# Shifted matmuls in place of a strided load, unit 0's means on VectorE, and longer planned landing times in an interleaved conv and FFN kernel

## Chip, cores, metric

One Trainium2 chip, one core of it. The metric is device time in microseconds of one execution of the whole program, from HBM inputs to HBM output; the time before is the median of 3 runs, 932.0 us (931.72 to 933.56). The profiled execution is one more run, of 932.73 us; its span, from the first to the last instruction of the trace, is 930.9 us.

## What is computed

Two layers, each a gated causal convolution (A) and a gated feed-forward block (B), each with a residual and a layer norm ahead of it, on S = 2048 tokens of D = 576 channels, with F = 4608 hidden units and 4 taps in the short convolution:

```python
def A(q, k, v, shift_k, ssm_k, ssm_D):
    k_pad = jnp.pad(k, ((0, 0), (ks - 1, 0), (0, 0)))
    k_shift = sum(k_pad[:, t:t + S, :] * shift_k[:, ks - 1 - t] for t in range(ks))
    kv = k_shift * v
    y = irfft(rfft(kv padded to 2S) * rfft(ssm_k padded to 2S))[:S]
    y = y + kv * ssm_D
    return q * y

def B(x, w_gate, w_up, w_down):
    return (gelu(x @ w_gate) * (x @ w_up)) @ w_down

x = A_q
x = x + A(layernorm(x), A_k, A_v, A_shift_k, A_ssm_k, A_ssm_D)
x = x + B(layernorm(x), B_w_gate, B_w_up, B_w_down)
x = x + A(layernorm(x), A_k, A_v, A_shift_k, A_ssm_k, A_ssm_D)
x = x + B(layernorm(x), B_w_gate, B_w_up, B_w_down)
```

The convolution's `y` does not depend on `x`, so both layers share it. All inputs and the output are bfloat16.

## The kernel before, in words

**Units.** The tokens are cut into four chunks of 512. A unit is one chunk in one layer: (layer 0, chunk 0), (0, 1), (1, 0), (1, 1), then the same of chunks 2 and 3, numbered 0 to 7. The weights are streamed in five passes over units [0], [1, 2], [3, 4], [5, 6], [7], and each pass has three phases, one per third of F. One visit of a unit in a phase is 12 up-projections `gu` (gate and up side by side, 18 matmuls each, L1435; GELU on ScalarE L1439, product into `hT` on VectorE L1440) and then four down-projections `dn` (L1452), one for each tile of 128 rows, added to the residual `x_c` on VectorE (L1488). Tokens lie on partitions as (p i): partition p holds the four consecutive tokens 4p to 4p+3.

**Convolution.** It is done in blocks of 512 tokens by a Fourier transform written as matmuls with twiddle tables `W` and `Wx`. Per block: load `k` and `v` (`load_k` L168, `load_v` L173); multiply the shifted keys by the taps on VectorE (`kvt`, L186 and L191) and by `v` (L196); transform (L222 and L260 on TensorE, `eo` on ScalarE, L237 to L251 on VectorE); multiply the spectra `kr` (of kv) and `hr` (of the filter), which are spilled to DRAM (`Kd`, `Hd`, L349) and loaded again (L459, L467), with L297 to L301; transform back (L339). The filter block is turned by DMA transposes (L369), written to DRAM (`Td`) and read again (L388).

**The head (`begin`).** Block 0 of the convolution and the first chunk's norm run before the first `gu`, in an order written out by hand. SP issues, in this order: `k`, `kx`, the filter's first block `hn` in two parts (L719, L720), `v`, `x_b` (the first chunk's input, L1006), half of the twiddles `W` (L736), `Wx`, the filter's second block, the other half of `W`, then the first FFN weights `wgu` (L991 to L993). ACT's queue issues `sk` and `dvec` (the taps and the skip weights). For the first 512 channels of block 0 the taps are applied by TensorE: `k` is transposed into `kT` (L769, evicted L771) and multiplied by diagonal matrices `dg` made from the taps (`shift_taps`, L662), and VectorE multiplies the PSUM result by `v` (L779). For the last DW = 64 channels (`taps_rest`) VectorE does it all, from `kx`: seven rows per partition, of which rows 3 to 6 are the partition's own four tokens (copied at L784) and rows 0 to 2 are the three tokens ahead of them, which are the last three tokens of partition p - 1. They come by a strided load of 127 x 3 pieces of 64 channels (L727). Partition 0 has zeros there (L724).

PSUM tiles in the head come from `ps()`, which gives three tiles of the pool `psp` and then one of the single-buffered `cpsp`, in turn.

**Unit 0's norm.** `gate0` makes the first layer's gated sum and its row sum `s` (L1288, L1291 on VectorE), `mean0` the negated mean `nm` (GpSimd, L1051, through `mean_after`), `sq0` the sum of squares (ScalarE, L1059), `root0` the reciprocal root `rstd` (GpSimd, L1066 and L1067), `norm0` the normalized tile `xn` (L1241), `turn0` its transposes (L1257) and `copy0` the eviction into `xnT` (L1264), which the first `gu` reads (L1360). Tiles 0 and 2 go first, 1 and 3 between the first half-width `gu`.

**The plan.** Everything else of the convolution and the norms is placed between the FFN's matmuls at build time. `Pace` counts a planned time for TensorE (`t.pe`), VectorE and ScalarE from the constants `C_*`; `fill` takes from the queues `L` (loads), `V` (VectorE operations), `Pq` (TensorE pieces) and `spills` whatever is ready at the planned time. A load is taken to have landed a fixed number of microseconds after its planned issue: `at["k"]` and `at["v"]` (9.0 each), `at[("ld", kt, a)]` for `kr` and `hr` (8.0), `hd_at` for a spilled spectrum (6.0). An operation is emitted no earlier than that. The emitted order is fixed; on the chip each engine takes its instructions in that order and waits on semaphores. The loads and spills above all go through GpSimd's queue, the weights and transposes through SP's.

Of the kernel before, what the change touches and what calls it, by code (L numbers as in the profile page):

```python
# [16 lines left out]
ALU = mybir.AluOpType  # L17
F32 = mybir.dt.float32
BF16 = mybir.dt.bfloat16
# [3 lines left out]
P = 128  # L23
# [3 lines left out]
RT = BS // P  # L27
# [57 lines left out]
class Conv:  # L85
# [261 lines left out]
    def spill(self, dst, t, ready=0.0, key=None):  # L347
        def run():
            self.nc.gpsimd.dma_start(out=dst, in_=t[:].rearrange("p s d -> p (s d)"))  # L349
            self.hd_at[key] = self.t.pe + 6.0  # L350
        self.spills.append((ready, run))

    def store(self, dst, t, ready):
# [57 lines left out]
    def step(self, m, kv=None, loaded=False):  # L411

        nc, D, t = self.nc, self.D, self.t
        kc, kr, hr, z, nyb, prs = {}, {}, {}, {}, {}, {}
        KTS = (0, 2, 1, 3)
        at = {}
# [5 lines left out]
        if not loaded:  # L422
            def lk():
                self.load_k(m, nc.gpsimd)
                at["k"] = t.pe + 9.0

            def lv():
                self.load_v(m, nc.gpsimd)
                at["v"] = t.pe + 9.0
            self.L.append((lambda: max(self.kv_at.get(m - 1, NEVER), self.td_at.get(self.NB - 1, NEVER)), lk))  # L430
            self.L.append((lambda: self.filt_at.get(m, NEVER), lv))
        else:
            at["k"] = at["v"] = 0.0
# [19 lines left out]
        def load(kt, a):  # L453
            def run():
                if a < m:
                    kr[(kt, a)] = (self.nkr % 3, self.krp.tile([P, 2, D], BF16, tag="kr", name="kr"))
                    self.kr_free[self.nkr % 3] = NEVER
                    self.nkr += 1
                    nc.gpsimd.dma_start(out=kr[(kt, a)][1][:].rearrange("p s d -> p (s d)"), in_=self.Kd[a][kt])  # L459
                if m == 1 and a == 0:  # L460
                    hr[(kt, a)] = (None, self.H1[:, kt, :, :])
                    at[("ld", kt, a)] = t.pe + 8.0
                    return
                hr[(kt, a)] = (self.nhr % N_HR, self.hrp.tile([P, 2, D], BF16, tag="hr", name="hr"))
                self.hr_free[self.nhr % N_HR] = NEVER
                self.nhr += 1
                nc.gpsimd.dma_start(out=hr[(kt, a)][1][:].rearrange("p s d -> p (s d)"), in_=self.Hd[m - a][kt])  # L467
                at[("ld", kt, a)] = t.pe + 8.0
            return run
        for kt, a in pairs:  # L470
            self.L.append((lambda a=a: max(self.hr_free[self.nhr % N_HR] if (m, a) != (1, 0) else 0.0,
# [120 lines left out]
        def inv(mt):  # L592
            def run():
                self.yb = nyb
                self.inverse(m, mt, self.terms(mt, z))
                done = t.on_act(C_EVA, t.pe + 0.98 + LAG)
                self.ps_free = done + LAG
                self.y_at[(m, mt)] = done + LAG
            return run
        zs = get(*[("z", kt, part) for kt in range(2) for part in range(2)])  # L600
        self.z_at[m] = zs
        out = [(lambda: max(zs(), self.y_used.get(m - 2, NEVER) if m > 1 else 0.0), 0.98, inv(mt), m) for mt in range(RT)]
# [92 lines left out]
    def begin(self, head, tables):  # L695

        tc, nc, D, KS = self.tc, self.nc, self.D, self.KS
        nd = D // P
        width = lambda db: min(P, D - db * P)
        with ExitStack() as es:  # L700
            tmp = es.enter_context(tc.tile_pool(name="s_tmp", bufs=1))
# [10 lines left out]
            dg = head.scratch([P, nd, RT, P], "dg")  # L712
            DW = D - nd * P
            kx = tmp.tile([P, RT + KS - 1, DW], BF16, name="kx")
            wx = [tmp.tile([P, RT, DW], BF16, name=f"wx{i}") for i in range(2)]

            def load_h(b):
                cols = slice(b * BS, (b + 1) * BS)
                nc.sync.dma_start(out=hn[b][:, 0:nd, :], in_=self.hk[0:nd * P, cols].rearrange("(b p) t -> p b t", p=P))  # L719
                nc.sync.dma_start(out=hn[b][0:D - nd * P, nd, :], in_=self.hk[nd * P:D, cols])  # L720

            nc.scalar.dma_start(out=sk1[:].rearrange("p d j -> p (d j)"), in_=self.sk.rearrange("d j -> (d j)").unsqueeze(0))
            self.load_k(0, nc.sync)
            nc.vector.memset(kx[:, 0:KS - 1, :], 0.0)  # L724
            base = self.k2[RT - KS + 1:RT - KS + 2, nd * P:nd * P + 1]
            row = base.ap[0][0]
            nc.sync.dma_start(out=kx[1:P, 0:KS - 1, :], in_=bass.AP(base.tensor, base.offset, [[RT * row, P - 1], [row, KS - 1], [1, DW]]))  # L727
            nc.scalar.dma_start(out=dvec[:], in_=self.sD.unsqueeze(0))
            nc.vector.memset(full[:], 1.0)
            nc.vector.memset(ones[:], 1.0)  # L730
            nc.vector.memset(kT[:, :, :, 0:2], 0.0)
            nc.scalar.activation(out=warm[:], in_=head.zero, func=ACT.Gelu_apprx_tanh)
            load_h(0)
            self.load_v(0, nc.sync)
# [17 lines left out]
            for db in range(nd + 1):  # L752
                nc.tensor.matmul(ps[0:width(db), 0, db:db + 1], lhsT=dvec[:, db * P:db * P + width(db)], rhs=ones[:, 0:1],
                                 start=True, stop=True)
# [6 lines left out]
                nc.gpsimd.tensor_tensor(out=hn[0][0:w, lo:hi, 0], in0=hn[0][0:w, lo:hi, 0], in1=dcol[0:w, lo:hi], op=ALU.add)  # L761

            k, v = self.kt_[0], self.vt_[0]
            DBS = [(0, 1), (2, 3)]
            for n, dbs in enumerate(DBS):
                pt = self.psp.tile([P, 2, 1024], BF16, tag="pr", name="kps")
# [6 lines left out]
            def taps(dbs):  # L773
                ps = self.ps()
                out = ps[:].rearrange("p e (i c) -> p e i c", i=RT)
                for e, db in enumerate(dbs):
                    self.shift_taps(k, kT, dg, P, db, out[:, e])
                vd = v[:, :, dbs[0] * P:dbs[0] * P + 2 * P].rearrange("p i (e c) -> p e i c", e=2)
                nc.vector.tensor_tensor(out=vd, in0=out[:], in1=vd, op=ALU.mult)  # L779

            def taps_rest():

                cols, tt = slice(nd * P, D), nc.vector.tensor_tensor
                nc.vector.tensor_copy(out=kx[:, KS - 1:, :], in_=k[:, 0:RT, cols])  # L784
                for j in range(KS - 1, -1, -1):
                    tt(out=wx[j < KS - 1][:], in0=kx[:, KS - 1 - j:KS - 1 - j + RT, :],
                       in1=self.skc[:, j, cols].unsqueeze(1).to_broadcast([P, RT, DW]), op=ALU.mult)
                    if j < KS - 1:
                        tt(out=wx[0][:], in0=wx[0][:], in1=wx[1][:], op=ALU.add)
                tt(out=v[:, :, cols], in0=wx[0][:], in1=v[:, :, cols], op=ALU.mult)  # L790

            def turn_h(b, hT, g):
                hv = hn[b][:].rearrange("p b (q i) -> p b i q", i=RT)
                pt = self.psp.tile([P, 2, 1024], BF16, tag="pr", name="hps")
                for i in range(2):
                    for db in range(nd + 1):
                        w = width(db)
                        nc.tensor.transpose(pt[:, i, db * P:db * P + w], hv[0:w, db, 2 * g + i, :], self.ident[0:w, 0:w])
                nc.scalar.copy(out=hT[:, 2 * g:2 * g + 2, :], in_=pt[:, :, 0:D])
# [48 lines left out]
            taps_rest()  # L848
            taps(DBS[0])
            head.stats(0)  # L850
            head.stats(1)
            turn_h(0, hT0, 0)
            turn_h(0, hT0, 1)
            taps(DBS[1])

# [40 lines left out]
            small = lambda: self.cpsp.tile([P, 2, 512], F32, tag="cps", name="cps")  # L896
# [38 lines left out]
def ssm_geglu_kernel(ctx, tc, A_q, A_k, A_v, A_shift_k, A_ssm_k, A_ssm_D, B_x, B_w_gate, B_w_up,  # L935
                     B_w_down, out):
    nc = tc.nc
    q2 = A_q[0]
    out2 = out[0]
    S, D = q2.shape  # L940
# [18 lines left out]
    t = Pace()  # L959
# [16 lines left out]
    small = pool("small", RT)  # L976
# [3 lines left out]
    conv = Conv(tc, ctx, t, A_k, A_v, A_shift_k, A_ssm_k, A_ssm_D, ident, psp, cpsp, ypool)  # L980
# [67 lines left out]
    def mean_after(v, when):  # L1048
        def run():
            v["nm"] = small.tile([P, 1], F32, tag=v["pfx"] + "nm", name="nm")  # L1050
            nc.gpsimd.tensor_scalar(out=v["nm"][:], in0=v["s"][:], scalar1=-1.0 / D, scalar2=None, op0=ALU.mult)  # L1051
            v["nm_at"] = max(t.pe, when) + C_TINY
        conv.spills.append((when - AHEAD, run))
# [85 lines left out]
    def g_sum(c, j):  # L1139

        v = hvars.setdefault(c, {})[j] = {"pfx": "g_"}
        v["s"] = small.tile([P, 1], F32, tag="s", name="s")
        return v
# [88 lines left out]
    with tc.manual_schedule():  # L1232
# [3 lines left out]
        vs0 = [{"pfx": "l_"} for _ in range(RT)]  # L1236
# [55 lines left out]
                                               accum_out=v["s"][:])  # L1292

        def mean0(j):
            mean_after(vs0[j], 0.0)
            conv.spills.pop()[1]()

        def sq0(j):
            square_task(lambda: x_c[0][:, j, :], vs0[j])
# [6 lines left out]
        def more(k):  # L1306
# [5 lines left out]
        head = SimpleNamespace(  # L1312
            zero=neghalf_t[:], more=more, stats=lambda j: [run() for _, _, run in g0[2 * j:2 * j + 2]],
            act_sum=act_sum0, act_sq=act_sq0, gate=gate0, mean=mean0, sq=sq0, root=root0, norm=norm0, turn=turn0, copy=copy0,
            scratch=lambda shape, name: xtp.tile(shape, BF16, tag="xnT", name=name),
            stay=lambda: xpool.tile([P, RT, 2, D], BF16, tag="x", name="H1"))
# [76 lines left out]
        for wb, ph, ui, first, final in visits:  # L1393
            layer, c = units[ui]
# [33 lines left out]
            for fi in range(FP if wb else 0):  # L1428
# [3 lines left out]
                for k in range(NKC):  # L1432
                    b = blk_of[k]
                    for s, r0 in ((0, 0), (1, HK)):
                        nc.tensor.matmul(pair[:, s, :], lhsT=w[r0:r0 + HK, k, gi * P:(gi + 1) * P],  # L1435
                                         rhs=xnT[r0:r0 + HK, b, :], start=(k == 0), stop=(k == NKC - 1))
# [8 lines left out]
            for j in range(RT):  # L1445
# [35 lines left out]
                elif end:  # L1481
                    v = g_sum(c, j)
# [60 lines left out]
```

## Time and profile before

| | |
|---|---|
| median of 3 runs | 932.0 us |
| profiled execution | 932.73 us, span 930.9 us |
| granted TensorE clock | 0.998 |
| start of the first `gu` (L1360) | 42.91 us |
| unit 1's first visit, first `dn` | from 187.5 us |
| unit 2's first visit, last `dn` | to 244.3 us |
| unit 4's first `gu` | 429.3 us |
| DMA moved | 130.30 MB, mean 140 GB/s |

A profile line names engine, kernel line, operation and tiles, written `out<-in`; times are microseconds from the start of the span. A row of the waits reads: who waited, `<-` for whom, total, how often, the longest. Engines are named as in the trace: PE is TensorE, DVE VectorE, ACT ScalarE, POOL GpSimd, SP SyncE; a `q` behind the name means its instruction queue.

### The profile page before, as it was taken

To read this page: it belongs to the slowest core of one execution; us is meant where nothing else is said; L and a number is where in the kernel's file an instruction comes from. 1 tells how busy PE (TensorE), PEld (TensorE's weight loads), DVE (VectorE), ACT (ScalarE), POOL (GpSimd) and SP (SyncE) were. 2 spreads that over 40 slices of the span, in tenths; PEclk is the share of its full clock that TensorE was granted. 3 is DMA by queue.
4 is the path that set the end of the run, shared out by engine and by line. 5 is a ranking of instruction groups with operands and counts; after the bars stand their busy time and mean duration, and the time that the engine had idled before them with its cause. 6 is when DMAs were issued, how large, how long until landed. Compare 5 with 4: busy or idle time off the path is not lost.

```text
span 930.9 us, 19353 instructions
## 1 busy us (share of the span) xinstructions
PE 917.3 (99%) x8246; PEld 533.5 (57%) x8246; DVE 591.2 (64%) x1058; ACT 291.9 (31%) x538; POOL 143.5 (15%) x305
## 2 busy tenths in 40 slices
PE   7999999999999999999999999999999999999998
PEld 5787556455564664645646646556556556556555
DVE  7888977577797888698988953662333335432332
ACT  5764224423215134342132222341221223221211
POOL 1443003302023012230202201230000003100000
PEclk9999999999999999999999999999999999999999
DMA  8988988938735904962942920790720730977620
GB/s 217 318 245 235 195 192 150 230 47 211 205 116 112 265 1 85 255 171 57 239 139 64 195 76 27 146 184 3 148 83 1 141 89 14 166 179 165 142 65 26
DMA packets 128872, 130.30 MB, mean 140 GB/s; under 512 B 43920, under 2 KB 120721, under 8 KB 128786
## 3 DMA queue, kind: packets, MB, share of 16 engines
q1 hardware_dynamic: 119614, 93.52, 47.4%
q0 software_dynamic: 9168, 35.54, 11.9%
q8 instruction: 64, 1.05, 0.5%
q14 instruction: 22, 0.18, 0.1%
q10 hardware_dynamic: 4, 0.01, 0.0%
HBM read 107.81 MB, written 11.80 MB: 128 GB/s over the span
## 4 chain that ended last, share of the span: by engine, by line
PE 88%; DMA 5%; issue 2%; DVE 2%; SPq 1%; ACT 1%; POOL 0%; POOLq 0%; DVEq 0%; ACTq 0%
PE gu L1435 53%; PE dn L1452 28%; PE gu L1360 3%; DMA v<-in_A_v_dram 2%; DMA k<-in_A_k_dram 1%; PE ps L211 1%; DMA hr<-Hd 1%; PE cps L339 1%; DMA Hd<-hc 1%; PE cps L222 1%; PE cps L260 1%; PE cps L211 1%; SPq L719 1%; ACT junk L1059 0%; POOL rstd L1067 0%
## 5 line engine op out<-in xcount | busy, mean ns | idle before, releaser
L1435 PE MATMUL gu<-xnT,wgu 64*128 64x512 bf16 x4968 | 541.2, 376 | 0.0
L1435 PEld LDWEIGHTS <-wgu 64*128 64x128 bf16 x4968 | 239.3, 94 | 294.5 <-issue 6.9
L1439 ACT ACTIVATE ga<-gu 128x512 f32<-128x512 f32 x276 | 164.8, 597 | 514.2 <-PE gu L1435 508.0
L1440 DVE TENSOR_TENSOR hT<-ga,gu 128x512 bf16<-128x512 f32 x276 | 189.3, 686 | 201.4 <-ACT ga L1439 199.9
L1452 PE MATMUL dn<-wd,hT 128*128 128x288 bf16 x2304 | 295.9, 287 | 2.7 <-DVE hT L1440 2.2
L1452 PEld LDWEIGHTS <-hT 128*128 128x128 bf16 x2304 | 224.1, 98 | 69.8 <-issue 10.5
L1488 DVE TENSOR_TENSOR x_c<-x_c,dn 128x576 f32<-128x576 f32 x64 | 48.2, 752 | 57.3 <-PE dn L1452 57.1
L1051 POOL TENSOR_SCALAR nm<-s 128x1 f32<-128x1 f32 x62 | 23.3, 376 | 303.3 <-DVE x_c L1483 199.7
L1059 ACT ACTIVATE junk<-x_c,nm 128x576 bf16<-128x576 f32 x48 | 37.0, 770 | 27.6 <-POOL nm L1051 27.6
L1067 POOL TENSOR_TENSOR rstd<-ve,neghalf_t 128x1 f32<-128x1 f32 x62 | 40.2, 649 | 5.2
L467 POOL DMA_DIRECT2D hr<-Hd x32 | 17.6, 550 | 123.0 <-DVE prod L300 117.4
L262 ACT COPY eo<-cps 128x576 f32<-128x576 f32 x32 | 20.5, 639 | 39.6 <-PE cps L260 31.2
L1474 DVE TENSOR_TENSOR ob<-x_c,dn 128x576 bf16<-128x576 f32 x15 | 11.3, 754 | 29.0 <-PE dn L1452 25.6
L1360 PE MATMUL gu<-xnT,wgu 64*128 64x256 bf16 x432 | 24.7, 269 | 0.5 <-DVE xnT L1264 0.5
L1360 PEld LDWEIGHTS <-wgu 64*128 64x128 bf16 x432 | 21.2, 94 | 3.4 <-issue 0.7
L301 DVE TENSOR_TENSOR prod<-prod 128x576 bf16<-128x576 bf16 x48 | 22.0, 458 | 1.7
L1066 POOL TENSOR_SCALAR ve<-ss 128x1 f32<-128x1 f32 x62 | 18.0, 290 | 30.4 <-ACT junk L1059 30.1
L186 DVE TENSOR_TENSOR kvt<-k,skc 128x1152 bf16<-128x1152 bf16 x24 | 17.7, 753 | 4.5 <-DMA k<-in_A_k_dram 4.3
L354 POOL DMA_DIRECT2D out_dram<-ob x12 | 6.6, 551 | 86.5 <-DVE ob L1474 82.8
L544 DVE TENSOR_TENSOR zs<-zs,prod 128x576 f32<-128x576 f32 x24 | 18.1, 754 | 0.3
L541 DVE TENSOR_TENSOR zs<-sum,prod 128x576 f32<-128x576 bf16 x24 | 18.1, 754 | 0.3
L315 DVE TENSOR_TENSOR yb<-zs 128x576 bf16<-128x576 f32 x24 | 17.1, 752 | 0.1
(143 smaller groups left out, 537.9 us busy)
## 6 DMA issues: line engine op xcount, KB each, us to landing
wgu<-in_B_w_gate_dram SPq DMA_DIRECT2D x45, 576.0 KB, 6.0
wd<-in_B_w_down_dram SPq DMA_DIRECT2D x30, 864.0 KB, 6.6
wgu<-in_B_w_up_dram SPq DMA_DIRECT2D x45, 512.0 KB, 7.8
hr<-Hd POOLq DMA_DIRECT2D x32, 288.0 KB, 5.7
kr<-Kd POOLq DMA_DIRECT2D x24, 288.0 KB, 6.1
Kd<-kc POOLq DMA_DIRECT2D x12, 288.0 KB, 4.0
k<-in_A_k_dram POOLq DMA_DIRECT2D x3, 1008.0 KB, 10.8
wgu<-in_B_w_up_dram SPq DMA_DIRECT2D x45, 64.0 KB, 7.4
```

The lines of the kernel that those rows point to most:

```text
L211: nc.tensor.matmul(ps[:, h, 0:HW], lhsT=self.fwd_w(kt, s, i), rhs=src[:, i, h * HW:(h + 1) * HW], start=(n == 0), stop=(n == RT - 1))
L262: nc.scalar.copy(out=A[i][:], in_=ps[:, :, 0:HW])
L301: nc.vector.tensor_tensor(out=dst, in0=pr[:, 0, :], in1=pr[:, 1, :], op=ALU.subtract if part == 0 else ALU.add)
L1051: nc.gpsimd.tensor_scalar(out=v["nm"][:], in0=v["s"][:], scalar1=-1.0 / D, scalar2=None, op0=ALU.mult)
L1059: nc.scalar.activation(out=junk[:], in_=get_x(), func=ACT.Square, bias=v["nm"][:, 0:1], accum_out=v["ss"][:])
L1067: nc.gpsimd.tensor_tensor(out=v["rstd"][:], in0=ve[:], in1=neghalf_t[:, 0:1], op=ALU.pow)
L1360: nc.tensor.matmul(pair[:, s, e * 256:(e + 1) * 256], lhsT=w[r0:r0 + HK, k, gi * P:(gi + 1) * P], rhs=xnT[r0:r0 + HK, blk_of[k], tok], sta ...
L1435: nc.tensor.matmul(pair[:, s, :], lhsT=w[r0:r0 + HK, k, gi * P:(gi + 1) * P], rhs=xnT[r0:r0 + HK, b, :], start=(k == 0), stop=(k == NKC - 1))
L1439: nc.scalar.activation(out=ga[:], in_=pair[:, 0, :], func=ACT.Gelu_apprx_tanh)
L1440: nc.vector.tensor_tensor(out=hT[:, fi, :], in0=ga[:], in1=pair[:, 1, :], op=ALU.mult)
L1452: nc.tensor.matmul(acc[:, h, 0:HW], lhsT=hT[:, fi, at * P:(at + 1) * P], rhs=wd[2 * wb + fi // WT][:, fi % WT, h * HW:(h + 1) * HW], start ...
L1488: nc.vector.tensor_tensor(out=xh, in0=xh, in1=acc[:, :, 0:HW], op=ALU.add)
```

## The change

Three edits.

1. The load of `kx`'s first three rows and the zeroing ahead of it go. A 128 x 128 matrix `below` is made instead: zeros in its first column, the identity shifted by one column in the others. Three matmuls with `below` as weights and 64 columns of `k`'s rows 1, 2 and 3 put partition p - 1's rows on partition p (and zeros on partition 0) in a PSUM tile `px`, and one VectorE copy brings them into `kx`. They stand ahead of the transposes of `k`, behind the `dvec` matmuls. `px` comes from `ps()`, so all later PSUM tiles of the head move on by one turn.
2. `mean0`, the negated means of unit 0's four tiles, runs on VectorE and no longer on GpSimd.
3. Four planned landing times are longer: `k` 14.0 for 9.0, `v` 11.0 for 9.0, spectra loads 9.0 for 8.0, spilled spectra 7.0 for 6.0.

```diff
@@ spill, step, load
-            self.hd_at[key] = self.t.pe + 6.0
+            self.hd_at[key] = self.t.pe + 7.0
...
                 self.load_k(m, nc.gpsimd)
-                at["k"] = t.pe + 9.0
+                at["k"] = t.pe + 14.0
...
                 self.load_v(m, nc.gpsimd)
-                at["v"] = t.pe + 9.0
+                at["v"] = t.pe + 11.0
...
-                    at[("ld", kt, a)] = t.pe + 8.0
+                    at[("ld", kt, a)] = t.pe + 9.0
...
-                at[("ld", kt, a)] = t.pe + 8.0
+                at[("ld", kt, a)] = t.pe + 9.0
@@ begin
             kx = tmp.tile([P, RT + KS - 1, DW], BF16, name="kx")
+            below = tmp.tile([P, P], BF16, name="below")
...
             self.load_k(0, nc.sync)
-            nc.vector.memset(kx[:, 0:KS - 1, :], 0.0)
-            base = self.k2[RT - KS + 1:RT - KS + 2, nd * P:nd * P + 1]
-            row = base.ap[0][0]
-            nc.sync.dma_start(out=kx[1:P, 0:KS - 1, :], in_=bass.AP(base.tensor, base.offset, [[RT * row, P - 1], [row, KS - 1], [1, DW]]))
             nc.scalar.dma_start(out=dvec[:], in_=self.sD.unsqueeze(0))
...
             nc.vector.memset(kT[:, :, :, 0:2], 0.0)
+            nc.vector.memset(below[:, 0:1], 0.0)
+            nc.vector.tensor_copy(out=below[:, 1:P], in_=self.ident[:, 0:P - 1])
...
             k, v = self.kt_[0], self.vt_[0]
+            px = self.ps()
+            for i in range(KS - 1):
+                nc.tensor.matmul(px[:, 0, i * DW:(i + 1) * DW], lhsT=below[:], rhs=k[:, RT - KS + 1 + i, nd * P:D], start=True, stop=True)
+            nc.vector.tensor_copy(out=kx[:, 0:KS - 1, :], in_=px[:, 0, 0:(KS - 1) * DW].rearrange("p (i c) -> p i c", c=DW))
@@ mean0
         def mean0(j):
-            mean_after(vs0[j], 0.0)
-            conv.spills.pop()[1]()
+            v = vs0[j]
+            v["nm"] = small.tile([P, 1], F32, tag="l_nm", name="nm")
+            nc.vector.tensor_scalar(out=v["nm"][:], in0=v["s"][:], scalar1=-1.0 / D, scalar2=None, op0=ALU.mult)
+            v["nm_at"] = 0.0
```

## The prediction

> **What bounds the kernel now.** I read the page first, then TensorE's waits over the whole span, then the SP queue and the chain of waits around each wait that the change touches.
>
> ```profile
> PE 917.3 (99%) x8246; PEld 533.5 (57%) x8246; DVE 591.2 (64%) x1058; ACT 291.9 (31%) x538; POOL 143.5 (15%) x305
> PE dn L1452 <- DVE hT L1440: 2.2, 2, 1.6
> PE cps L260 <- ACT eo L262: 1.6, 1, 1.6
> PE ps L744 <- DVE full L729: 1.6, 1, 1.6
> PE ps L222 <- DMA W<-twiddles: 1.5, 1, 1.5
> PE cps L222 <- DVE v L779: 1.1, 1, 1.1
> PE xps L1257 <- DVE xn L1241: 0.6, 1, 0.6
> PE gu L1360 <- DVE xnT L1264: 0.5, 1, 0.5
> ```
>
> TensorE is busy 99% of the span. Its waits sum to 10.4 us (these rows and four smaller ones of 1.3 together), so no edit that leaves the matmuls alone can win more than that, and every edit has to be read at one of these waits. The clock is granted at 0.998 throughout.
>
> ```profile
> 1.19 0.32 SPq L727 DMA_DIRECT2D kx<-in_A_k_dram  x1
> 1.56 4.70 SPq L719 DMA_DIRECT2D hn<-in_A_ssm_k_dram  x1
> 6.91 0.58 SPq L173 DMA_DIRECT2D v<-in_A_v_dram  x1
> 4.00:5.00 1.00, 0.79 (x8) 0.25 (x5) 0.76 (x1) 0.62 (x2) 0.00 (x0) 1.00 0.09 14
> 8.00:9.00 1.00, 1.00 (x7) 0.71 (x6) 0.93 (x4) 0.00 (x0) 0.00 (x0) 1.00 1.04 361
> ```
>
> The first three rows are the SP queue (start, duration), the last two are one-microsecond windows, whose last two columns are DMA share and GB/s. The 48 KB load `kx` holds the filter load `hn` in issue for 4.70 us; the second `hn` load, of equal shape, takes 0.52. Meanwhile the DMA moves 14 GB/s where it later moves 361. The packet records say why: `kx` is 381 packets of 128 bytes that follow one another every 9.4 ns from 3.56 to 7.29 us, and the first `hn` packet starts at 6.93, although `k`'s last started at 3.61.
>
> ```profile
> 38.27 0.57 POOL L1067 TENSOR_TENSOR rstd<-ve,neghalf_t 128x1 f32<-128x1 f32 x1
> 38.83 0.22 POOL L1051 TENSOR_SCALAR nm<-s 128x1 f32<-128x1 f32 x1
> 39.08 0.78 ACT L1059 ACTIVATE junk<-x_c,nm 128x576 bf16<-128x576 f32 x1 [1.11 <-POOL nm L1051]
> 175.75 13.52 DMA k<-in_A_k_dram
> 217.68 6.98 DMA Hd<-hc
> 224.94 8.32 DMA hr<-Hd
> 379.61 9.38 DMA v<-in_A_v_dram
> ```
>
> The first three rows: tile 2's mean stands in POOL's queue behind tile 0's `rstd`, and ScalarE idles 1.11 us for it. The last four, from the chain, are landing times, where the plan of before assumes 9, 6, 8 and 9 us. VectorE works in order, so a planned use that comes before the landing blocks what follows it.
>
> **First stretch, 0 to 18 us.** Removed: the `kx` load and a memset of 0.14 us. The `hn` packets can then follow `k` at 3.6 instead of 6.9, and everything behind moves by some 3.0 us: `v` lands at 9.8 (12.82 now), `x_b` at 11.3 (14.26), the first twiddles at 12.4 (15.42 with `Wx`).
>
> Added on TensorE: three matmuls on 64 columns, which no row shows. The five `dvec` matmuls take 0.40 us (0.08 each), the sixteen 128-column transposes at L769 take 1.89 (0.12 each): 0.24 to 0.35, and I take 0.3, nearer to the transposes because each also loads 128 weights. VectorE gains a copy for `below`, about 0.2 us (COPY 128x256 takes 0.22), in its idle 1.31 us before `skc` at 3.03, and an eviction of 192 columns. That last is 0.25 us scaled from the 0.76 of 576 columns, at least the 0.18 of a 64-column copy. It fits between `dg`, which ends at 6.73, and the `kT` eviction, which waits for the transposes. Without that gap it would cost itself. `px` also takes one turn of the PSUM rotation, so the two tap groups swap `cps` and `ps`. Walking the slots, each is evicted before its next matmul.
>
> Walking VectorE's row from there: `kT` ends at 8.0 (0.3 later than now), `kx` copy 0.22 and seven tap operations 2.1 end at 10.3; L790 0.29; L779 1.14; both `stats` groups 2.47; the second L779 1.14: 15.4. TensorE ends its second tap group at 14.1 and three groups of L222 at 15.55, so the fourth starts there instead of at 18.00: 2.5 us won if nothing else moves. From 18.0 to 40.5 TensorE has no gap over 0.05 us, so this carries over. The weights for n=4 land at 45.8 and would be needed near 49.
>
> One thing can move: L753, which waits now for `dvec`, issued from ACT at 1.28. Its packet started only at 4.31, behind 75 `kx` packets. Afterwards `hn` stands there, 32 packets per engine at 46 ns: after `k`'s end at 3.8, `dvec` would start at 5.3 and L753 at 5.7 instead of 4.74. TensorE and VectorE are then 1.0 late and 1.6 us are won. Bounds: not held at all, 2.5; held behind `v` too (8 packets of 180 to 380 ns, to 8.4), 4.1 late and 1.5 lost. I take 1.6, nearest to what the row shows, a small packet held by the load issued just before it.
>
> [...]
>
> **Unit 0's means.** On VectorE the mean of tile 2 follows its sum directly, which ends at 38.15; a 128x1 operation there takes 0.21 (L1024). ScalarE is free from 37.97, so `junk` starts at 38.4 instead of 39.08, and the chain behind it (POOL 0.42 and 0.57, `xn`, `xps`, `xnT`, first `gu` at 42.91) moves by 0.7. L1288 of tile 1 ends at 40.39, just ahead of the new `xn` at 40.46. For tile 0 nothing changes: ScalarE is in `y` until 36.55. Tiles 1 and 3 lie beside matmuls: nothing, and 0.2 us each of VectorE is not waited for. 0.7 us; bounds 0 and 0.7.
>
> **The plan.** Order of the instructions, with TensorE's work counted between them. The first `kvt` of block 2 stands 2.2 up-projections later (4.3 us): VectorE reaches it at 189.3 instead of 185.0, as `k` lands (189.27). It also stands behind the last `hT` of its unit, so the next matmuls no longer queue behind it: both waits on `hT`, 2.2 us, go. The first product of block 2 stays behind the same `hT`, but two kv operations (1.5 us) come before it and its second part (1.2 us) moves behind the next unit. So VectorE waits 1.5 instead of 3.0 for `hr`, ends that part 1.25 earlier (234.6), and of the 1.64 at L260 some 0.3 stay: 1.3 won. Bounds: 0.3, if the wait there follows the load alone, and 1.6. Block 3's `v` use moves 12.75 us behind its load, where 9.4 is needed; that wait was 0.05. No matmul is added. All later uses have 9.8 us or more, where before 7.8 was enough.
>
> What is late next: block 2's fourth inverse stands some 11 us of matmul work later, but the last `xn` of unit 4 stands where it stood, and its transposes land at 415 for a start at 429.3.
>
> **Sum.** 1.6 + 0.7 + 2.2 + 1.3 = 5.8 us. The profiled execution took 932.7 (span 930.9), which gives 926.9; it lies 0.7 over the median of the runs, 932.0, so the forecast is 926.2.
>
> **Rivals.**
> - `dvec` isn't held: 2.5 instead of 1.6, 925.3. For it: its packet is one of 1152 bytes on its own queue. Against: the 3.0 us now. [...]
> - The first stretch gives nothing: `dvec` held behind `v`, or `hn` slow for its own 576 packets. 1.6 less, 927.8; with the bound of 1.5 lost 929.3. For it: the wgu issue at 17.18 also hangs 3.50 us, without `kx`. Against: the second `hn`.
> - The plan only moves its two waits, because landings vary (`k` took 13.5 us here, 7.8 for block 3) and later uses have less margin: 3.5 less, 929.7.
> - Slower: unit 4 starts late. Block 2's kv work and filter work are pushed into the end of unit 2 (hc, ob and eo operations of 5.2 us in a row). If the fourth inverse delays `xn` of unit 4, TensorE waits at 429.3 once the delay passes the 14 us between 415 and there; past 20 us it takes back the 5.8, at 24 us the time is 936. For it: the 11 us. Against: `xn`'s unmoved place.
>
> **Chances.** Forecast 0.46, `dvec` free 0.25, first stretch empty 0.13, plan moves its waits 0.10, slower 0.06. The range 924.3 to 930.4 holds all but the slower case and the tails: its low end takes the bounds 2.5, 0.7, 2.2 and 1.6 (925.0) and 0.7 us of scatter, its high end is the third rival with as much. About 0.2%, 1.9 us, can be told from no change here. Faster 0.90, same 0.04, slower 0.06.
>
> **What would show it.** No `hn` issue over 1 us and 300 GB/s from 3.6 us on; L753's wait shows `dvec`; the fourth L222 at 16.4 (held) or 15.5; the first `gu` near 40.6. No wait of `dn` on `hT` near 190, under 0.5 us at L260 near 240. Wrong would be a new TensorE wait over 1 us at 429 or in the first 18 us, or `hn` still slow in issue.

## The result, and the profile after

The changed kernel takes 925.01 us (median of 5 runs, 924.81 to 926.42) where the kernel before took 931.72 beside it (5 runs, 928.71 to 933.56): a ratio of 0.9934 with a 95% interval from 0.9913 to 0.9955. The forecast was 926.2. The profiled execution took 924.81 us with a span of 923.0, so the span is 7.9 us shorter than that of before (930.9). Line numbers behind the edits differ by up to 5 from those of before: L1360 is now L1365, L1435 L1440, L1452 L1457, L1241 L1244; in the head some are lower (L729 is now L726, L753 L752).

The page's row of busy times, then all rows of TensorE's waits over the span (who waited, for whom, total, times, longest):

```profile
PE 915.1 (99%) x8248; PEld 534.6 (58%) x8249; DVE 592.1 (64%) x1064; ACT 291.6 (32%) x538; POOL 143.4 (16%) x301
```

```profile
PE ps L743 <- DVE full L726: 1.5, 1, 1.5
PE xps L1260 <- DVE xn L1244: 0.8, 1, 0.8
PE dn L1457 <- DVE ob L1466: 0.5, 1, 0.5
PE gu L1365 <- DMA wgu<-in_B_w_up_dram: 0.5, 1, 0.5
PE ps L765 <- ACT skc L749: 0.4, 1, 0.4
PE gu L1440 <- DVE x_c L1488: 0.4, 1, 0.4
PE cps L260 <- ACT eo L262: 0.3, 1, 0.3
PE cps L662 <- ACT kT L774: 0.3, 1, 0.3
```

The waits of `dn` on `hT` and both waits of the first stretch at L222 are gone, the one at L260 has fallen from 1.6 to 0.3, and two small ones are new: `px` at 5.11 waits 0.37 until ScalarE has copied `skc` out of its PSUM buffer, and a `gu` at 347.24 waits 0.36 for `x_c`. The first `gu` waits as long as before; its row names a load of `wgu` now, but it starts 0.14 us behind the end of `xnT`'s copy, where it started 0.15 behind it before. But TensorE's busy time has also fallen, by 2.2 us, although it has two recorded matmuls more. The waits alone can't explain that.

The first `hn` load in the SP queue (start, duration), and the two one-microsecond windows (busy time of PE, PEld, DVE, ACT, POOL with counts, granted clock, DMA share, GB/s):

```profile
1.18 0.42 SPq L720 DMA_DIRECT2D hn<-in_A_ssm_k_dram  x1
```

```profile
4.00:5.00 1.00, 0.73 (x7) 0.41 (x6) 0.67 (x1) 0.62 (x3) 0.00 (x0) 1.00 1.11 385
8.00:9.00 1.00, 1.00 (x6) 0.67 (x5) 0.90 (x4) 0.00 (x0) 0.00 (x0) 1.00 0.97 389
```

`hn` is issued in 0.42 us where it hung 4.70, and between 4 and 5 us the DMA moves 385 GB/s where it moved 14. The transforms back of tile 2 (L339) start at 32.47 and not at 35.16, so 2.7 us are won there; the first `gu` starts at 39.91 and not at 42.91, 3.0.

The first two products with the taps in block 2 (`kvt`), before and after:

```profile
189.30 1.43 DVE L186 TENSOR_TENSOR kvt<-k,skc 128x1152 bf16<-128x1152 bf16 x2 [4.28 <-DMA k<-in_A_k_dram]
```

```profile
185.83 1.42 DVE L186 TENSOR_TENSOR kvt<-k,skc 128x1152 bf16<-128x1152 bf16 x2
```

Before, VectorE idled 4.28 us for `k` there, and `hT` stood behind it; after, it doesn't wait. The chain's rows for the spectra of block 2 (start, length from issue to landing) are as long as before:

```profile
210.48 6.99 DMA Hd<-hc
217.76 8.23 DMA hr<-Hd
```

The landing took as long as ever; only its user has moved behind it. Most of the missing 2.2 us of busy time is in three rows. These are three windows of 3.41 us in the kernel before, around the two waits for `k`:

```profile
190.08:193.49 3.41, 1.23 (x10) 0.54 (x8) 3.38 (x6) 0.64 (x1) 0.00 (x0) 1.00 0.54 101
193.49:196.90 3.41, 3.41 (x15) 2.11 (x16) 3.34 (x6) 0.00 (x0) 0.00 (x0) 0.50 0.00 0
196.90:200.30 3.40, 3.40 (x30) 2.69 (x29) 3.29 (x8) 0.00 (x0) 0.00 (x0) 1.00 0.00 0
```

In the first, TensorE works for 1.23 us and idles for 2.18 (the two waits on `hT`). In the second it is busy throughout, but does 15 matmuls and not 30: the granted clock is 0.50. So that stall cost its 2.18 us and 1.7 more (half of 3.41) behind it; below, two runs test whether the half clock follows from it. The kernel after has no such stretch. The difference of these two spans then adds up: 3.0 at the first `gu`, 2.2 of waits near 190, 1.7 of half clock, 1.3 at L260, less the 0.4 at 347, is 7.8 of 7.9 us.

### The profile page after: what moved, and what is told of

Same layout as the page of the kernel before. It is cut to its first block, busy times and chain, and to the rows that moved or that the text cites. A ratio compares the mean times of both kernels' runs of the same rounds, so it can differ in the third digit from the quotient of the medians.

```text
span 923.0 us, 19358 instructions
## 1 busy us (share of the span) xinstructions
PE 915.1 (99%) x8248; PEld 534.6 (58%) x8249; DVE 592.1 (64%) x1064; ACT 291.6 (32%) x538; POOL 143.4 (16%) x301
## 4 chain that ended last, share of the span: by engine, by line
PE 91%; DMA 5%; DVE 1%; SPq 1%; POOL 1%; issue 0%; ACT 0%; DVEq 0%; ACTq 0%
PE gu L1440 57%; PE dn L1457 29%; PE gu L1365 3%; DMA wgu<-in_B_w_up_dram 2%; PE cps L339 1%; DMA hn<-in_A_ssm_k_dram 1%; DMA hr<-Hd 1%; DMA Hd<-hc 1%; PE cps L260 1%; PE cps L222 1%; DMA k<-in_A_k_dram 0%; SPq L996 0%; POOL rstd L1070 0%; SPq L995 0%; ACT junk L1062 0%
## 5 line engine op out<-in xcount | busy, mean ns | idle before, releaser
L1440 PE MATMUL gu<-xnT,wgu 64*128 64x512 bf16 x4968 | 541.5, 376 | 0.4 <-DVE x_c L1488 0.4
L1440 PEld LDWEIGHTS <-wgu 64*128 64x128 bf16 x4968 | 240.6, 94 | 293.7 <-issue 7.5
L1445 DVE TENSOR_TENSOR hT<-ga,gu 128x512 bf16<-128x512 f32 x276 | 189.1, 686 | 201.7 <-ACT ga L1444 200.2
L1457 PE MATMUL dn<-wd,hT 128*128 128x288 bf16 x2304 | 293.8, 286 | 0.5 <-DVE ob L1466 0.5
L1457 PEld LDWEIGHTS <-hT 128*128 128x128 bf16 x2304 | 223.6, 98 | 66.1 <-issue 10.5
L1365 PE MATMUL gu<-xnT,wgu 64*128 64x256 bf16 x432 | 24.7, 269 | 0.5 <-DMA wgu<-in_B_w_up_dram 0.5
L1365 PEld LDWEIGHTS <-wgu 64*128 64x128 bf16 x432 | 21.2, 94 | 3.4 <-issue 0.7
L1097 DVE SCALAR_TENSOR_TENSOR x_c<-g_t,rstd,x_c 128x576 f32<-128x576 f32 x16 | 13.1, 817 | 8.2 <-POOL rstd L1070 8.1
## 6 DMA issues: line engine op xcount, KB each, us to landing
k<-in_A_k_dram POOLq DMA_DIRECT2D x3, 1008.0 KB, 10.5
```

The costliest lines, as they stand in the source:

```text
L1365: nc.tensor.matmul(pair[:, s, e * 256:(e + 1) * 256], lhsT=w[r0:r0 + HK, k, gi * P:(gi + 1) * P], rhs=xnT[r0:r0 + HK, blk_of[k], tok], sta ...
L1445: nc.vector.tensor_tensor(out=hT[:, fi, :], in0=ga[:], in1=pair[:, 1, :], op=ALU.mult)
L1457: nc.tensor.matmul(acc[:, h, 0:HW], lhsT=hT[:, fi, at * P:(at + 1) * P], rhs=wd[2 * wb + fi // WT][:, fi % WT, h * HW:(h + 1) * HW], start ...
```

## The experiments

Each was timed against the kernel before in the same job: the first four on one chip, where the kernel before took 931.28 (19 runs); the load in two parts, the means, the moved sum and the first fill on a second, 929.22 (15 runs); the rest on a third, 931.3 (14 runs). Of these 48 executions of the kernel before, 10 show a mean granted clock of 0.998 or 0.996, one or two windows at half clock, and none of those on the second chip does. So the half clock of the profiled execution is not in most executions of the kernel before, and a median holds little of its 1.7 us.

**The plan alone, and `k` alone.** The first has the four landing times and nothing else, the second only that of `k`.

```diff
-            self.hd_at[key] = self.t.pe + 6.0
+            self.hd_at[key] = self.t.pe + 7.0
...
-                at["k"] = t.pe + 9.0
+                at["k"] = t.pe + 14.0
...
-                at["v"] = t.pe + 9.0
+                at["v"] = t.pe + 11.0
...
-                    at[("ld", kt, a)] = t.pe + 8.0
+                    at[("ld", kt, a)] = t.pe + 9.0
...
-                at[("ld", kt, a)] = t.pe + 8.0
+                at[("ld", kt, a)] = t.pe + 9.0
```

> The kernel before with the four longer landing times alone. Theory (the plan's two waits, and the half clock of 3.41 us that follows the first of them in the profile of before): 2.2 + 1.7 + 1.3 less a new wait of 0.4 at an up-projection near 347 us, so 4.8 us under the kernel before. Rival (the plan's waits only move, the gain is the head's): within 1 us of it. The trace should show full clock from 9 to 930 us by the theory.

> The kernel before with the landing time of k at 14.0 alone. Theory (wait and half clock are one cause): 3.9 us under the kernel before and no half clock near 193 us; the wait of 1.6 at L260 stays. Rival (the half clock has nothing to do with the wait): 2.2 us under it, half clock still there.

Measured: 928.41 for the four, ratio 0.9970 (0.9960 to 0.9980), and 927.98 for `k` alone, 0.9967 (0.9955 to 0.9980). These are the same: the other three landing times add nothing that could be measured. By the ratios 2.8 and 3.1 us are won, less than the 4.8 and 3.9 expected, which counted 1.7 us of half clock that most executions of the kernel before don't have. In the run with `k` alone, no `dn` waits for `hT`, and the wait at L260 reads:

```profile
PE cps L260 <- ACT eo L262: 0.2, 1, 0.2
```

The wait at L260 was expected to stay without the longer landing times of the spectra. It went: moving the `kv` operations is what took VectorE's work out of its way. The new wait of a `gu` on `x_c`, 0.37 us at 350.3, also belongs to `k`'s edit.

In the profiled run of the plan alone TensorE waited 2.51 us for `W` in the first stretch, which has nothing to do with the edit. The full clock from 9 us on that was expected did not come; the clock answered as near 190 in the kernel before:

```profile
13.07:16.48 3.41, 1.19 (x10) 0.59 (x7) 2.37 (x5) 0.52 (x1) 0.00 (x0) 1.00 0.99 352
16.48:19.89 3.41, 3.12 (x14) 1.98 (x15) 3.31 (x9) 1.32 (x3) 1.12 (x2) 0.50 1.10 247
```

**The head alone.** The changed kernel with the four old landing times (the diff above, reversed).

> The changed kernel with the four landing times of before: shifted matmuls and means on VectorE alone. Theory: the first up-projection at 39.9 instead of 42.9 us, so 3.0 us under the kernel before, with the wait of TensorE near 190 us and the half clock behind it still there. Rival (the head moves, but the plan of before gives it back at its waits): less than 1.5 us.

Measured: 926.9, 0.9957 (0.9943 to 0.9972), which is 4.0 us by the ratio, 1.0 more than expected. Its profile's wait on `eo` is back, 1.55 us at 235.95:

```profile
PE cps L260 <- ACT eo L262: 1.6, 1, 1.6
```

The waits on `hT` and the half clock behind them, expected to be still there, are not back in that run. `k` landed 10.5 us behind its issue (13.5 in the kernel before), VectorE idled 1.8 us for it and not 4.3, and no `dn` had to wait. So the stall for `k` comes and goes between executions of one plan, and part of what the head alone won beyond the 3.0 expected can be that. Head and plan multiply to 0.9927, whole change 0.9934: they add up within their intervals.

**The strided load kept.** The changed kernel, with the old load issued in its old place into a tile that nobody reads.

```diff
             self.load_k(0, nc.sync)
+            kold = tmp.tile([P, KS - 1, DW], BF16, name="kold")
+            base = self.k2[RT - KS + 1:RT - KS + 2, nd * P:nd * P + 1]
+            row = base.ap[0][0]
+            nc.sync.dma_start(out=kold[1:P, :, :], in_=bass.AP(base.tensor, base.offset, [[RT * row, P - 1], [row, KS - 1], [1, DW]]))
```

> The changed kernel, with the strided load of 381 pieces issued in its old place as well, into a tile that nothing reads. Theory (the load holds what is issued behind it): 2.7 us over the changed kernel, hn again about 4.7 us in issue, first up-projection at 42.6. Rival (the gain came from the means and from VectorE's shorter start): under 0.5 us over it.

Measured: 927.57, 0.9959 (0.9945 to 0.9974); by the ratios 2.3 us of the change's gain are given back (2.7 expected; the two intervals overlap slightly, at 0.9945 to 0.9955). The first `gu` starts at 42.91, 3.0 later than in the changed kernel. The SP queue and TensorE's largest wait of that run:

```profile
1.18 0.32 SPq L728 DMA_DIRECT2D kold<-in_A_k_dram  x1
1.55 5.00 SPq L720 DMA_DIRECT2D hn<-in_A_ssm_k_dram  x1
```

```profile
PE ps L222 <- DMA W<-twiddles: 1.9, 1, 1.9
```

The load alone, with no reader, holds the next load in issue for 5.00 us. What it brings doesn't matter, only that it stands there.

**The load in two parts.** The changed kernel without `below`, `px` and their copies; the rows are loaded again, but as 112 and 15 partitions. The load is shown beside that of the kernel before.

```diff
-            nc.sync.dma_start(out=kx[1:P, 0:KS - 1, :], in_=bass.AP(base.tensor, base.offset, [[RT * row, P - 1], [row, KS - 1], [1, DW]]))
+            for p0, n in ((1, 112), (113, 15)):
+                nc.sync.dma_start(out=kx[p0:p0 + n, 0:KS - 1, :],
+                                  in_=bass.AP(base.tensor, base.offset + (p0 - 1) * RT * row, [[RT * row, n], [row, KS - 1], [1, DW]]))
```

> The changed kernel without the shifted matmuls: kx's first rows are loaded again, the same 381 pieces of 128 bytes in the same place, but as two loads of 112 and 15 partitions instead of one of 127. Theory (what holds the queue is that all 381 pieces go through one DMA engine, and 112 and 15 partitions spread over more): within 0.5 us of the changed kernel, hn under 1 us in issue. Rival (it is the number of small pieces): 2 us or more over it, hn 4 us or more in issue.

Measured: 924.15, 0.9947 (0.9934 to 0.9959), first `gu` at 39.53. The SP queue:

```profile
1.18 0.99 SPq L728 DMA_DIRECT2D kx<-in_A_k_dram  x2
2.21 0.41 SPq L719 DMA_DIRECT2D hn<-in_A_ssm_k_dram  x1
```

The same bytes in two loads hold nothing: `hn` is issued in 0.41 us. The packets tell the two apart: in the kernel before, the 381 of the whole load follow one another every 9.4 ns, never more than two of them under way, with a DMA share of 0.09 of 16 engines (4 to 5 us), worth 1.4 engines. The two parts leave no such stretch: their 381 packets start within 1.32 us (3.37 to 4.69), where they took 3.72. That fits the expectation's theory; the records do not name a packet's engine, so that the whole load went through one is an estimate from the share.

**Means on GpSimd.** The changed kernel with `mean0` as before.

```diff
-            v["nm"] = small.tile([P, 1], F32, tag="l_nm", name="nm")
-            nc.vector.tensor_scalar(out=v["nm"][:], in0=v["s"][:], scalar1=-1.0 / D, scalar2=None, op0=ALU.mult)
-            v["nm_at"] = 0.0
+            mean_after(vs0[j], 0.0)
+            conv.spills.pop()[1]()
```

> The changed kernel with unit 0's means on GpSimd again. Theory from the trace after (of the 0.7 us that the means were to win, the next rstd, 1.13 us instead of 0.57, gave back 0.4): 0.3 us over the changed kernel. Rival (the prediction's term): 0.7 us over it.

Measured: 924.83, 0.9950 (0.9937 to 0.9964), beside 0.9934 (0.9913 to 0.9955) for the whole change: too little to tell by time. Its first `gu`, at 40.94, is 1.03 later, but an estimated 0.6 of that comes from the clock, full from 10.45 us here and from 9.28 there (the last section). A length inside the chain leaves that shift out: from the end of tile 2's sum to the start of its `xn` it took 2.99 us in the kernel before (38.15 to 41.14) and 2.99 here, 2.68 in the changed kernel (35.47 to 38.15). So the means won 0.3, not 0.7. Tile 2's `rstd` in the kernel before, then GpSimd's rows in the changed kernel, then VectorE's beside them (start, duration):

```profile
40.53 0.57 POOL L1067 TENSOR_TENSOR rstd<-ve,neghalf_t 128x1 f32<-128x1 f32 x1
```

```profile
36.70 0.19 POOL L1069 TENSOR_SCALAR ve<-ss 128x1 f32<-128x1 f32 x1 [0.55 <-ACT junk L1062]
36.98 1.13 POOL L1070 TENSOR_TENSOR rstd<-ve,neghalf_t 128x1 f32<-128x1 f32 x1
```

```profile
36.89 0.81 DVE L1291 SCALAR_TENSOR_TENSOR x_c<-x_b,mv,y 128x576 f32<-128x576 bf16 x1
```

Tile 2's `rstd` takes 1.13 us where it took 0.57, and it starts while VectorE is in the first step of tile 1's gated sum. `ve` is shorter, 0.19 for 0.42: in the kernel before it was `ve` (40.03) that started beside that step (39.58 to 40.39).

**That sum moved.** The changed kernel with the first step of tile 1's gated sum (L1291) behind tile 2's copy.

```diff
-            head.gate(1, None, 0)
             head.norm(2)
...
             head.copy(2, nc.vector.tensor_copy, nc.scalar.copy)
+            head.gate(1, None, 0)
```

> The changed kernel with VectorE's first step for tile 1 (L1291, 0.81 us) moved from ahead of tile 2's xn to behind its copy into xnT. Theory (GpSimd's rstd of tile 2 takes 1.13 instead of 0.57 us because it runs beside that VectorE instruction): rstd back at 0.57, first up-projection at 39.4 instead of 39.9, 0.5 us under the changed kernel. Rival (the rstd varies by itself): same time, rstd anywhere from 0.57 to 1.1.

Measured: 923.71, 0.9941 (0.9928 to 0.9953), first `gu` at 39.35. By time it can't be told from the whole change (0.9934); the lengths in the chain tell. Tile 2's `rstd`:

```profile
37.00 0.55 POOL L1070 TENSOR_TENSOR rstd<-ve,neghalf_t 128x1 f32<-128x1 f32 x1
```

It starts within 0.02 us of where it did and takes 0.55; from sum to `xn` it is 2.11 us. With VectorE out of the way 0.88 is won: 0.65 by the mean, near the 0.7 forecast, and 0.23 by `ve`. And the wait at L1260 falls from 0.83 to 0.25.

**The changed kernel again, and the two best edits together.** The first is unaltered; the second has the load in two parts and the moved sum.

> The changed kernel once more, unaltered, beside the two runs of the same job that are compared with it. Expected: 924.8 us +- 0.7, first `gu` near 39.9, tile 2's `rstd` 1.13 us beside VectorE's L1291 again, no half-clock stretch behind 40 us. If tile 2's `rstd` came to 0.57 here, the long one was chance and not VectorE's neighbour.

> The changed kernel with two of the tested edits together: the rows ahead loaded by a strided load in two parts of 112 and 15 partitions (no shifted matmuls, no `below`, no `px`), and tile 1's gated sum moved behind tile 2's copy. Theory: one edit acts before 6 us, the other at 37 us, on the same chain, so their gains add: first `gu` at 39.53 - 0.56 = 39.0, time some 0.9 us under the changed kernel of the same job. Rival: the chain to the first `gu` is limited behind 16 us by something that neither touches (the transforms' operands), so that the first `gu` stays at 39.35 as with the moved sum alone and only 0.5 is won.

Measured: 925.32 (924.17 to 926.16), 0.9931 (0.9911 to 0.9952), and 924.12 (923.96 to 924.63), 0.9920 (0.9898 to 0.9943). `rstd` of tile 2 took 1.14 in the first and 0.55 in the second, so the long one is no chance. The first `gu` came at 39.47 and 39.28; 39.0 was expected. The clock has to be taken out first: in three profiles the first `gu` came 0.44 us later for 0.89 and for 0.91 us by which full clock began later (the last section), and half is taken here. The combined run has no clock record, but its matmuls show the clock: those of 128 columns start 0.107 us apart until 9.7 and 0.056 behind. Put to the changed kernel's 9.28 us, the first `gu` is by estimate at 39.75 with the load in two parts (full clock from 8.84), 39.32 with the moved sum (9.34) and 39.07 with both, where 39.91 less the two gains is 39.16. So within 0.1 us the two gains add, and that 39.28 lies near the 39.35 of the moved sum alone comes from the clock. By time the combined kernel is the shortest against the kernel before, 1.2 us under the changed kernel (0.9 expected), but their intervals overlap.

**The wait filled, first try.** The kernel before, with 14 matmuls into an unread tile ahead of the last `dn` group that waits.

```diff
+                    if wb == NP and ui == 1 and j == 0 and fi == FP - 1:
+                        idle = cpsp.tile([P, 2, 512], F32, tag="cps", name="idle")
+                        for _ in range(14):
+                            nc.tensor.matmul(idle[:, 0, 0:HW], lhsT=ident[:], rhs=conv.skc[:, 0, 0:HW], start=True, stop=True)
```

> The kernel before with 14 matmuls of 288 columns (1.7 us) into a PSUM tile that nothing reads, put in front of the down-projection that waits 1.64 us for the last hT near 193 us: the wait stays, TensorE is busy in it. Theory (TensorE's own idle time brings the half clock): 1.7 us under the kernel before, full clock at 193 to 197 us. Rival (the half clock comes from elsewhere, or from the wait of VectorE): same time as the kernel before, half clock still there.

Measured: 930.54, 1.0011 (1.0002 to 1.0020), where 1.7 us under the kernel before was expected. It tells nothing of the clock: in the profiled run `k` landed 11.9 us behind its issue, VectorE idled 3.1 us, and the 1.88 us of added matmuls covered what TensorE would have waited: the last `hT` ended at 193.67 and the `dn` ahead of it at 192.55, an estimated 1.1 us. The clock stayed at 1.00, but there was no long wait to fill.

**A certain wait, idle and filled.** So `k` was made later: a copy of 590 KB that nobody reads stands ahead of it in GpSimd's queue. The second kernel also has 30 and 12 unread matmuls ahead of the two groups that wait.

```diff
+        self.spare = tc.dram_tile([P, RT * D], BF16, name="spare")
...
+                if m == 2:
+                    nc.gpsimd.dma_start(out=self.spare, in_=self.k2[0:BS, :].rearrange("(p i) d -> p (i d)", i=RT))
                 self.load_k(m, nc.gpsimd)
...
+                    if wb == NP and ui == 1 and j == 0 and fi >= FP - 2:
+                        idle = cpsp.tile([P, 2, 512], F32, tag="cps", name="idle")
+                        for _ in range(30 if fi == FP - 2 else 12):
+                            nc.tensor.matmul(idle[:, 0, 0:HW], lhsT=ident[:], rhs=conv.skc[:, 0, 0:HW], start=True, stop=True)
```

> The kernel before with one edit: block 2's `k` load stands behind a 590 KB copy that nobody reads in the same queue, so that `k` lands some 3 us later and the two waits of `dn` on `hT` near 190 are certain and longer (2.2 -> about 5 us in all). Theory (the clock halves for 3.41 us behind a stretch of 3.41 us in which TensorE idles most of the time): a granted clock of 0.50 for at least 3.4 us right behind the waits, so the time is longer by the added wait plus 1.7 for each such stretch: about 934 to 936. Rival (the half clock seen once was not tied to the wait): the clock stays 1.00 and only the wait is added, about 932 to 933.

> As the run with the later `k`, but TensorE gets 30 and 12 matmuls of 128 x 288 into an unread PSUM tile (0.134 us each, so 4.0 and 1.6 us) ahead of the two `dn` groups that wait, and so isn't idle there. VectorE's stall is the same. Theory: no half clock, so this run is about 1.7 us or more below the run with the idle wait, though it computes 5.6 us more (it stands in the waits). Rival: the clock halves all the same (then its cause is not TensorE's idleness), and the time is equal or up to 3 us longer.

Measured: 937.41 (935.17 to 939.61), 1.0063 (1.0041 to 1.0085), with the idle wait; 935.79 (934.10 to 938.52), 1.0049 (1.0032 to 1.0066), with the filled one. The first lies above the 934 to 936 that were expected. The medians differ by 1.6 us where the theory gives 1.7 or more, but the intervals overlap, and `k` landed 1.9 us earlier in the filled profile; the conclusion rests on the profiles and the clocks. With the idle wait (4.13 and 1.40 us on `hT`), four windows of 3.41 us:

```profile
191.48:194.89 3.41, 0.00 (x0) 0.00 (x0) 1.43 (x3) 0.36 (x1) 0.00 (x0) 1.00 1.28 173
194.89:198.30 3.41, 1.36 (x6) 0.57 (x7) 3.34 (x6) 0.00 (x0) 0.00 (x0) 0.50 0.06 12
198.30:201.71 3.41, 3.41 (x16) 2.18 (x15) 3.38 (x5) 0.00 (x0) 0.00 (x0) 0.50 0.00 0
201.71:205.10 3.39, 3.39 (x29) 2.72 (x28) 2.95 (x7) 0.00 (x0) 0.00 (x0) 1.00 0.00 0
```

An idle window is followed by one at half clock; that one is idle for 2.05 us, and half clock goes on; the third is busy, and the clock is full again. The first 52 `dn` matmuls behind the waits, idle and then filled (start, duration):

```profile
197.60 8.54 PE L1455 MATMUL dn<-wd,hT 128*128 128x288 bf16 x52 [1.40 <-DVE hT L1443]
```

```profile
197.00 6.53 PE L1455 MATMUL dn<-wd,hT 128*128 128x288 bf16 x52
```

The same work takes 2.0 us less where TensorE had been kept busy, although VectorE idled 6.29 us for `k` there too. The filled profile has no clock record, but its matmuls start 0.122 us apart from 191.6 to 204 us, where those of the idle one start 0.240 apart until the clock is full again at 201.7. The shorter stall alone hardly explains the full clock: by the end of the `hT` it waited for (193.63), an unfilled TensorE would have idled an estimated 2.5 us of one window (the one from 191.16, counted on from 10.25, where the matmuls of that run become fast), more than the 2.05 to 2.22 us that were followed by half clock in other profiles. The mean clocks of all executions point the same way, but not cleanly: with the idle wait four of five show 0.996 and one 0.998, with the filled one four of eight still show 0.998. Where that window lay isn't on record. So in the two profiles the half clock follows TensorE's idleness; filling did not keep it away in every execution.

## Why the prediction was right, and where its terms were off

| step | forecast, us | measured in the profiles, us |
|---|---|---|
| first stretch | 1.6 | 2.7 (L339 at 32.47, was 35.16) |
| unit 0's means | 0.7 | 0.3 |
| both waits for `k` | 2.2 | 2.2 and 1.7 of half clock |
| L260 | 1.3 | 1.3 (0.34 left of 1.64) |
| new wait at 347 | 0 | -0.4 |
| sum | 5.8 | 7.8 of 7.9 |

The direction and the places of the terms held, and 925.01 lies in the range; three sizes were off. That the number came within 1.2 us is in part luck: by the medians below the head won 1.7 more than forecast and the plan 0.7 less. The last column is that of two profiled executions, of which the one before had the half clock.

*The first stretch.* The term was mis-sized at "I take 1.6, nearest to what the row shows, a small packet held by the load issued just before it". `dvec` was not held by `hn`: its packet started at 3.76, not 5.3, though `hn`'s packets had started at 3.54, and L752 ran at 4.33. That is the first rival, whose 925.3 came closest. The row had been misread. The 3.0 us from `dvec`'s issue (1.28) to its packet (4.31) were taken for a hold by `kx`, but without `kx` `dvec` needed 2.49 all the same (1.27 to 3.76), so `kx`'s part was some 0.5 us. What the 2.49 are stays open: `sk` and `k`, the first loads of the two queues, had their first packets 0.9 and 1.0 us after issue, and the second loads 2.2 to 2.5, about when the last of `k`'s packets started (3.61 before, 3.88 after). Whether `k` held them was not tested. In the changed kernel `dvec` came 0.22 us behind `hn`'s first packet, in the kernel before 0.74 us behind `kx`'s first, when 69 of `kx`'s packets had started (the prediction counts 75). The fourth L222 started at 15.23, near the 15.5 given for this case. The other parts stood: three `px` matmuls 0.32 us (0.3 forecast), the copy for `below` 0.18 (0.2), the eviction 0.35 (0.25), in the gap where it was put. Only "each is evicted before its next matmul" was wrong: `px` waited 0.37 us for its PSUM buffer; the transposes of `k` behind it still started only 0.17 later than before (5.24 for 5.07).

*The means.* "The chain behind it (POOL 0.42 and 0.57 ...) moves by 0.7" took `rstd` as 0.57, but the shorter chain brought it beside VectorE's L1291, and it took 1.13 (and `ve` 0.19 for the 0.42). The run with the sum moved shows it: 0.55, and 0.88 us won in all. Beside that step of tile 1, tile 2's `rstd` took 1.13 us (changed kernel) and 1.14 (the same again, and with the load in two parts); with the step moved it took 0.55 twice. Why it is longer there isn't shown.

*`k`.* Both waits went as forecast, with the later `kvt`. What I did not see is the half clock behind them. "The clock is granted at 0.998 throughout" was the sentence that hid it: it wasn't throughout, and so the 10.4 us of waits were no cap on the gain either. One window of 3.41 us at half clock out of 931 is a mean of 0.998. The new wait of 0.36 at 347, which the prediction lacked, is `k`'s too. The gain is also less steady than one profile says: the profiled execution before, 932.73, lay high among its runs (928.71 to 933.56), and in the head alone's profile, with the old landing times, `k` was there early enough for no such wait. With the new landing times VectorE still idled 1.0 and 1.3 us for `k` in two profiles (means on GpSimd, moved sum), but no `dn` waited. By the medians the plan won 2.8 us and not 3.5, and the head 4.0 and not 2.3.

*L260.* 1.3 as forecast, and by the mechanism given (VectorE's `kv` operations), not by the spectra's longer landing times, which weren't needed.

*The rivals.* The plan didn't only move its waits, and unit 4 was not late: no wait over 0.4 us stands between 40 and 917. What stays open is why `k`, the same load each time, took from 7.4 (strided load kept) to 13.9 us (moved sum) to land; no run was made for that.

## What to carry to other kernels

A small load can cost what stands behind it in its queue, not its bytes: here 48 KB held the next load in issue for 4.70 us, and 0.41 when it came in two parts. Look for an issue of several microseconds right behind it, and for a way to cut it that spreads (112 and 15 partitions in place of 127), before work is added on another engine. Before the time from an issue to its first packet is called a hold by one load, compare it with a load in the same place without that one. And look at the clock behind a stall of TensorE, in as many executions as have it: in the kernel before 2.18 us of idleness were followed by 3.41 us at half clock, 1.7 us that a mean clock of 0.998 hid.

## What the runs showed of the hardware

**Idle stretches of TensorE and the clock behind them.** A clock record lists the states of the clock with their lengths. In the kernel before and in the changed kernel all lengths but that of the last state are multiples of 3.413 us (3.413 is one, 184.32 is 54, 733.87 is 215, 914.77 is 268), so the windows here have that length and are counted on from full clock's start. A window with 2.18 (kernel before) or 2.22 us (plan alone) of idle TensorE was followed by one at half clock; in the run with the later `k` one with 2.05, itself at half clock, was followed by another. One with 1.86 us was followed by one at 1.00 (the strided load kept):

```profile
12.71:16.13 3.42, 1.56 (x14) 0.95 (x13) 2.37 (x5) 0.84 (x1) 0.00 (x0) 1.00 1.03 374
```

What idleness between these does was not measured. Nor was each busy window followed by full clock: with the load in two parts TensorE is busy throughout from 2.02 to 5.43 us, mostly with one-row matmuls, and the next window is still slow (matmuls of 128 columns start 0.107 us apart there, until 8.8).

**Where full clock begins, and the first `gu`.** The records begin with the first full clock; ahead of it the windows above print 1.00, but the matmuls are slow: in the changed kernel the transposes of `k` with 128 columns start 0.107 us apart ahead of 9.28 us, and others of that width 0.056 behind it, so I read half clock there. Full clock began at 9.28 us in the changed kernel, 8.39 in its second profile, and 10.19 with the head alone; the first `gu` followed at 39.91, 39.47 and 40.35, which is 0.44 us for 0.89 and for 0.91. By these numbers a start later by a whole window of 3.41 us is an estimated 1.7 us of scatter that no edit of the kernel explains; the five runs of the changed kernel spread over 1.6, but that this is the cause isn't shown. A difference of less than that between two profiles is read here from lengths inside the chain, as with the means above.
